# A hand-written issue list carried into the second quarter of an attention + two-layer kernel, with idle transposes ahead of the first work

## The chip, the cores and the metric

One core of a Trainium2 chip runs the kernel. The metric is device time in microseconds (us) of one execution, as the median of three runs; lower is better. The engines are named as in the profile: PE is TensorE's matmul, PEld its weight load, DVE is VectorE, ACT is ScalarE, POOL is GpSimd, SP the engine that issues the DMAs. Each engine executes its own queue in order, and waits on semaphores for the others.

## The reference, cut to what matters

```python
def _attn_ref(x, state):                       # x 4x8x512x64, state 4x8x32x64
    scores = scale * np.matmul(x, state.transpose(0, 1, 3, 2))
    a = softmax(scores)                        # with + 1e-09 in the divisor
    xread = np.matmul(a, state)
    scores2 = scale * np.matmul(state, x.transpose(0, 1, 3, 2))
    a2 = softmax(scores2)
    sread = np.matmul(a2, x)
    return np.concatenate([xread, sread], axis=2)

def _moe_ref(x, w_in, w_out, alpha):           # 2304 tokens, 512 -> 2048 -> 512
    h = x @ w_in
    g = np.maximum(h, 0.0) + alpha * np.minimum(h, 0.0)
    return g @ w_out

def _moe2_ref(x, w_in, w_out):
    h = x @ w_in
    g = np.maximum(h, 0.0) + np.log1p(np.exp(-np.abs(h)))
    return g @ w_out
```

The attention's output, as 2304 rows of 512, goes through the first layer and then the second. The weights arrive as 64-bit floats.

## The kernel before, in words

**Stages.** The 2048 hidden columns of a layer are cut into four quarters of 512 (NQ = 4). A quarter is worked off in blocks: the four batches b = 0 to 3 (512 tokens each, in four column pieces fc of 128 hidden columns) and one block B of 128 rows, the state's rows of all batches. For each piece, `hidden` makes a 128x512 bank of hidden values on PE, `act` applies the layer's function on ACT and DVE and splits the result into a high and a low part (g), and `out_part` multiplies g with the output weights: 12 matmuls of 512 columns, as high x high, low x high and high x low (`mm3`, lines 173 to 175). In the first layer the state is multiplied into the weights first (`sw_products`, line 305), so a hidden bank is 6 matmuls.

**Weights.** 64 weight tiles (`wsrc`: 4 input and 4 output tiles for each quarter and layer) are loaded as 64-bit numbers into staging buffers (`wload`, three buffers and one extra), and turned to 32-bit floats in five operations: a on ACT (two instructions, lines 246 and 247), j, f and v on DVE (lines 251, 257 and 261), g on POOL (line 267). Output tiles are then split into high and low (h on ACT, l on POOL). Tiles 0 to 7 belong to the first quarter, 8 to 15 to the second, 16 to 23 to the third.

**Order.** The attention and the whole first quarter are issued in the order of a list, ORDER, inside `tc.manual_schedule()`. It has 405 steps. A step is a letter with a number; each letter is a small function in `steps()`:

- x, y load the tokens, L loads a weight tile, P loads alpha (all on SP's queue)
- s, S make scores of one or two groups (8 groups of 4 heads), on PE; k copies them (ACT)
- t, m, u, e, z, n, b, c, d turn, reduce, exponentiate, normalise and split the scores for xread; M, E, Z, T, K, R, F, X, W do sread (M and Z on DVE; T, R and X on PE; E, K, F and W on ACT)
- w, p, q multiply the state into input weights (PE) and split the product (ACT, DVE)
- H, A, C, G, D, O, Q are the blocks of the first layer: hidden bank (PE), relu (ACT), prelu (DVE), high part (ACT), low part (DVE), output product (PE), copy of the output (ACT). I, J and H16 are the row block B.

`LOW_POOL` and `SUB_POOL` name the groups whose d and u go to POOL instead of DVE.

All that follows the list, from the second quarter on, is written as loops and ordered by the framework's scheduler, which goes by its own cost model. It may issue an instruction of the loops ahead of steps of the list, on any engine, where it thinks that it is ready sooner. In the loops, `out_part` lags three pieces behind (`LAG`), `wconv` converts one tile ahead where it can, `wprep` (as often as `SPLIT_SECOND` or `SPLIT` name the running piece n) takes a tile over, and `sw_batch` makes the next quarter's products at pieces 10, 13 and 15, and the fourth one at piece 1 of the quarter itself.

PSUM is two pools of four banks: psa (scores, hidden, products) and psb (outputs, and the first two groups' scores).

Of the kernel before, what the change touches and what calls it, by code (L numbers as in the profile page):

```python
# [18 lines left out]
P = 128  # L19
# [26 lines left out]


ORDER = """
x0 P0 L0 L1 x1 x2 L2 L3 s0 a0 k0 j0 a1 t0 M0 f0 E0 m0 s1 T0 k1 j1 e0 v0 K0 f1 L4 g0 z0 v1 a2 n0 t1 L5 g1 Z0
b0 m1 x3 B0 j2 a3 u1 f2 M1 e1 c0 v2 E1 d0 j3 L6 T1 S2 g2 K1 z1 k2 f3 n1 a4 Z1 v3 t2 g3 k3 j4 a5 w00 m2 f4 u2  # L50
w01 b1 p00 j5 p01 H0 v4 f5 L7 g4 e2 x4 q01 c1 H1 A0 d1 v5 h4 C0 a6 l4 w03 z2 G0 j6 A1 n2 D0 p03 C1 g5 O0 f6
G1 a7 D1 v6 h5 b2 g6 H2 t3 c2 j7 l5 h6 m3 H3 A2 f7 l6 C2 u3 O1 G2 v7 A3 e3 D2 g7 C3 z3 G3 O2 h7 D3 n3 d2 l7
M2 x5 y0 L8 b3 E2 w02 q03 c3 O3 p02 d3 Z2 x6 L9 L10 q02 y1 M3 H4 Q3 S4 A4 R0 k4 C4 k5 y2 H5 t4 G4 t5 F0 a8
D4 X0 T2 m5 O4 A5 m4 u5 K2 C5 E3 u4 e5 Z3 e4 j8 H6 G5 z5 W0 a9 R1 D5 n5 R2 z4 A6 O5 F1 b5 n4 F2 C6 c5 j9 G6
b4 X1 D6 X2 c4 H7 W2 d5 d4 W1 f8 T3 A7 H8 M4 K3 C7 E4 O6 v8 G7 Z4 A8 L11 g8 x7 D7 C8 a10 f9 M5 H9 v9 G8 E5
j10 L12 g9 O7 A9 D8 Z5 a11 C9 f10 v10 G9 S6 Q7 j11 L13 g10 y3 y4 D9 H10 f11 v11 k7 O8 k6 g11 t7 a12 t6 m7
a13 m6 O9 u7 A10 u6 e7 C10 e6 z7 G10 H11 z6 n7 D10 R3 n6 A11 b7 T5 y5 F3 L14 T4 C11 c7 X3 b6 O10 K4 d7 W3 M7
c6 j12 K5 d6 M6 G11 E7 D11 R4 E6 f12 H12 Z7 y6 F4 v12 Z6 L15 g12 j13 T6 A12 R5 h12 X4 C12 O11 K6 l12 f13 G12
W4 F5 D12 a14 v13 X5 R6 W5 L16 g13 y7 j14 T7 F6 H13 Q11 f14 v14 H14 L17 g14 A13 K7 C13 X6 O12 A14 G13 C14 W6
D13 G14 D14 R7 H15 F7 h14 l14 X7 A15 w10 h13 C15 W7 O13 l13 G15 p10 D15 q10 I0 J0 H16 A16 C16 G16 D16 w11  # L60
w12 p11 p12 q11 q12
""".split()

BY_PE = (0,)

LOW_POOL = (1, 4, 6, 7)
SUB_POOL = (2, 5)

SPLIT_SECOND = (2, 2, 3, 4, 5, 7, 9, 10, 16)
SPLIT = (1, 2, 4, 5, 7, 9, 10, 16)  # L70

SW_AHEAD = (10, 13, 15)
# [5 lines left out]
def mixer_kernel(  # L78
# [313 lines left out]
    def out_part(m, q, b, fc, g, take=True):  # L392

        gh, gl = g
        if b == B:
            ps = bank(psb)
            for c in range(4):
                f = slice(c * P, (c + 1) * P)
                mm3(ps, gh[:, f], gl[:, f], *weight("o", m, q, c), c == 0, c == 3)
            out_take(m, q, b, 0, ps)  # L400
            return
        if fc == 0:
            for j in range(4):
# [42 lines left out]
    def steps():  # L446
# [228 lines left out]

        @step
        def H(i):
            b, fc = divmod(i, 4)
            if b == 0:
                ps = live["H", i] = bank(psa)  # L680
                for k in range(2):
                    nc.tensor.matmul(
                        ps, sw[0][k][0].f[:, fc * P : (fc + 1) * P], at0_at[k].f, start=k == 0, stop=k == 1
                    )
            elif b < B:
                live["H", i] = hidden(0, 0, b, fc)
# [17 lines left out]

        @step
        def C(i):
            prelu(0, *divmod(i, 4), live["A", i], live["H", i])

        @step
        def G(i):  # L710
# [7 lines left out]

        @step
        def O(i):  # L720
            out_part(0, 0, *divmod(i, 4), live["G", i], take=False)

        @step
        def Q(i):
            for j in range(4):
                out_take(0, 0, i // 4, j, yps[j])

        for x_ in ORDER:
            do[x_[0]](int(x_[1:]))
# [72 lines left out]
```

## Time and profile before

| what | us |
|---|---|
| median of three runs (lowest, highest) | 750.41 (748.25, 751.65) |
| the profiled execution, its own time | 751.67 |
| its span in the trace | 749.9 |
| PE busy in it | 714.9 (95%) |
| DVE, ACT and POOL busy | 448.6, 423.2, 183.9 |

The span runs from the first to the last instruction in the trace. Busy is time in which an engine executes; the granted clock is TensorE's, as a share of 2.4 GHz. A timeline row reads: start, duration, engine, line, operation, what it writes and reads, count, and in square brackets the idle time before it with what ended it.

### The profile page before, as it was taken

To read this page: it belongs to the slowest core of one execution; us is meant where nothing else is said; L and a number is where in the kernel's file an instruction comes from. 1 tells how busy PE (TensorE), PEld (TensorE's weight loads), DVE (VectorE), ACT (ScalarE), POOL (GpSimd) and SP (SyncE) were. 2 spreads that over 40 slices of the span, in tenths; PEclk is the share of its full clock that TensorE was granted. 3 is DMA by queue.
4 is the path that set the end of the run, shared out by engine and by line. 5 is a ranking of instruction groups with operands and counts; after the bars stand their busy time and mean duration, and the time that the engine had idled before them with its cause. 6 is when DMAs were issued, how large, how long until landed. Compare 5 with 4: busy or idle time off the path is not lost.

```text
span 749.9 us, 9339 instructions
## 1 busy us (share of the span) xinstructions
PE 714.9 (95%) x3516; PEld 556.6 (74%) x3516; DVE 448.6 (60%) x697; ACT 423.2 (56%) x765; POOL 183.9 (25%) x150
## 2 busy tenths in 40 slices
PE   3699987699999999999999999999999999999998
PEld 1267764387778777778888888888888888888886
DVE  4989977758668456974596224853267332333433
ACT  4769885735355234754587547864466454544560
POOL 2643433403024002652482004500044000000000
PEclk9799999799999999999999999999999999999999
DMA  7324653304012000320031001310020000001103
GB/s 263 116 81 166 202 171 116 107 2 141 28 49 92 0 1 29 118 79 1 29 112 57 1 0 57 122 48 1 1 59 26 0 1 1 0 1 57 56 15 112
DMA packets 16653, 47.25 MB, mean 63 GB/s; under 512 B 2016, under 2 KB 2016, under 8 KB 16608
## 3 DMA queue, kind: packets, MB, share of 16 engines
q1 hardware_dynamic: 16608, 46.66, 18.9%
q8 instruction: 27, 0.44, 0.2%
q14 instruction: 18, 0.15, 0.1%
HBM read 42.20 MB, written 4.46 MB: 62 GB/s over the span
## 4 chain that ended last, share of the span: by engine, by line
PE 82%; DVE 7%; DMA 4%; ACT 4%; issue 1%; POOL 1%; SPq 0%; ACTq 0%; DVEq 0%
PE pb L174 15%; PE pb L175 15%; PE pb L173 15%; PE pa L173 11%; PE pa L175 11%; PE pa L174 11%; DMA stg<-w1i 2%; DVE top L251 2%; PE pa L341 1%; DVE cnv L261 1%; PE pa L305 1%; ACT exp L246 1%; DMA acc<-xs 1%; ACT top L247 1%; DVE pa L372 1%
## 5 line engine op out<-in xcount | busy, mean ns | idle before, releaser
L386 DVE SCALAR_TENSOR_TENSOR pa<-pa,tmp 128x512 f32<-128x512 f32 x68 | 47.4, 697 | 127.6 <-ACT tmp L385 127.6
L429 DVE TENSOR_TENSOR acc<-pb,acc 128x512 f32<-128x512 f32 x102 | 67.3, 684 | 37.0 <-PE pb L175 37.0
L383 ACT ACTIVATE tmp<-pa 128x512 f32<-128x512 f32 x68 | 40.6, 597 | 85.2 <-PE pa L175 65.7
L267 POOL TENSOR_TENSOR cnv<-top,cnv 128x512 f32<-128x512 bf16 x48 | 59.2, 1233 | 67.8 <-DVE cnv L261 66.4
L251 DVE SCALAR_TENSOR_TENSOR top<-stg,top 128x512 uint16<-128x512 uint16 x63 | 58.1, 922 | 24.8 <-ACT top L247 24.6
L372 DVE SCALAR_TENSOR_TENSOR pa<-tmp,rest,pa 128x512 f32<-128x512 f32 (+1 forms) x80 | 53.4, 669 | 26.5 <-ACT tmp L380 22.9
L246 ACT ACTIVATE exp<-stg 128x512 bf16<-128x512 bf16 x63 | 42.1, 668 | 39.2 <-DMA stg<-w1i 9.7
L380 ACT ACTIVATE tmp<-pa 128x512 f32<-128x512 f32 x51 | 30.0, 595 | 42.2 <-PE pa L175 35.6
L261 DVE SCALAR_TENSOR_TENSOR cnv<-stg,exp 128x512 f32<-128x512 uint32 x48 | 43.8, 913 | 16.3 <-POOL wo5l L182 4.0
L247 ACT ACTIVATE top<-exp,top_bias 128x512 uint16<-128x512 uint16 x64 | 46.0, 719 | 5.0 <-POOL cnv L267 1.5
L385 ACT ACTIVATE tmp<-tmp 128x512 f32<-128x512 f32 x68 | 42.9, 632 | 1.8
L384 ACT ACTIVATE tmp<-tmp 128x512 f32<-128x512 f32 x68 | 43.0, 632 | 1.5
L257 DVE TENSOR_SCALAR exp<-top 128x512 uint16<-128x512 uint16 x64 | 37.4, 584 | 1.1
L179 ACT ACTIVATE g3h<-pa 128x512 fp32r<-128x512 f32 x29 | 17.3, 597 | 20.3 <-DVE pa L372 11.1
L179 ACT ACTIVATE g1h<-pa 128x512 fp32r<-128x512 f32 x29 | 17.3, 597 | 19.6 <-DVE pa L386 11.2
L182 DVE TENSOR_TENSOR g3l<-pa,g3h 128x512 fp32r<-128x512 f32 x29 | 20.0, 689 | 14.0 <-ACT g3h L179 13.7
L179 ACT ACTIVATE g0h<-pa 128x512 fp32r<-128x512 f32 x28 | 16.7, 597 | 20.0 <-DVE pa L386 10.6
L182 DVE TENSOR_TENSOR g2l<-pa,g2h 128x512 fp32r<-128x512 f32 x29 | 19.9, 687 | 12.0 <-ACT g2h L179 12.0
L182 DVE TENSOR_TENSOR g1l<-pa,g1h 128x512 fp32r<-128x512 f32 x29 | 19.9, 688 | 10.2 <-ACT g1h L179 9.8
L179 ACT ACTIVATE g2h<-pa 128x512 fp32r<-128x512 f32 x29 | 17.3, 597 | 13.9 <-DVE pa L386 7.2
L182 DVE TENSOR_TENSOR g0l<-pa,g0h 128x512 fp32r<-128x512 f32 x28 | 19.3, 688 | 9.2 <-ACT g0h L179 8.9
L182 POOL TENSOR_TENSOR wo3l<-cnv,wo3h 128x512 fp32r<-128x512 f32 x4 | 5.2, 1290 | 73.3 <-ACT wo3h L179 73.3
(903 smaller groups left out, 2157.8 us busy)
## 6 DMA issues: line engine op xcount, KB each, us to landing
stg<-w1o SPq DMA_DIRECT2D x16, 511.8 KB, 3.8
stg<-w2i SPq DMA_DIRECT2D x16, 511.8 KB, 3.9
stg<-w2o SPq DMA_DIRECT2D x16, 511.8 KB, 3.3
stg<-w1i SPq DMA_DIRECT2D x15, 511.8 KB, 5.1
acc<-xt SPq DMA_DIRECT2D x16, 256.0 KB, 4.4
out<-acc SPq DMA_DIRECT2D x16, 256.0 KB, 2.0
acc<-xs SPq DMA_DIRECT2D x8, 256.0 KB, 4.6
wo6h<-xs SPq DMA_DIRECT2D x4, 256.0 KB, 5.2
```

Of the source, the lines that this page charges most:

```text
L173: nc.tensor.matmul(ps, lh, rh, start=start, stop=False)
L174: nc.tensor.matmul(ps, lh, rl, start=False, stop=False)
L175: nc.tensor.matmul(ps, ll, rh, start=False, stop=stop)
L179: nc.scalar.activation(h, src, AF.Copy)
L182: eng_l.tensor_tensor(out=l, in0=src, in1=h, op=ALU.subtract)
L246: nc.scalar.activation(e, words(i)[0].bitcast(BF16), AF.Abs)
L247: nc.scalar.activation(t.bitcast(U16), e.bitcast(U16), AF.Relu, bias=top_bias, scale=TOP_SCALE)
L251: nc.vector.scalar_tensor_tensor(out=tu, in0=words(i)[0], scalar=TOP_SIGN, in1=tu, op0=ALU.bitwise_and, op1=ALU.bitwise_or)
L261: nc.vector.scalar_tensor_tensor(out=a, in0=words(i)[1], scalar=REST, in1=parts(i)[1], op0=ALU.mult, op1=ALU.mult)
L267: nc.gpsimd.tensor_tensor(out=a, in0=parts(i)[0], in1=a, op=ALU.add)
L372: nc.vector.scalar_tensor_tensor(out=ps[:, cs], in0=t[:, cs], scalar=a, in1=ps[:, cs], op0=ALU.mult, op1=ALU.add)
L429: nc.vector.tensor_tensor(out=a, in0=ps, in1=a, op=ALU.add)
```

## The change

The list is written anew: 449 steps instead of 405. It goes on past the first quarter's last block to the first batch block of the second quarter: new are H17 to H20 with their A, C, G, D, the outputs O14 to O17, the conversion of tile 15 (a15 to l15), the load L18, and w13, p13, q13 (the second quarter's last product). `BLOCKS` maps a step's number to quarter, block and piece. The loop over the second quarter starts at block 1, piece 4. `SPLIT_SECOND` has eight entries instead of nine, since one tile more is ready.

From the last instruction of the list on each of the five engines, `tc.issue_after` ties what follows: it is issued behind that instruction on that engine. It is an order of issue, not a wait for its end.

A new step N makes a number of 128x128 transposes of the identity into a bank of psb that nobody reads: N12 ahead of s0, N13 ahead of t0, N10 ahead of T0, N4 ahead of s1, N13 ahead of b0, N29 ahead of S2 and N26 ahead of w00, 107 in all. The d of groups 3 and 5 goes to POOL, and the u of group 2 to DVE.

In the diff a part of the old list is left out.

```diff
--- before.py
+++ after.py
@@ -46,27 +46,30 @@
 
 
 ORDER = """
-x0 P0 L0 L1 x1 x2 L2 L3 s0 a0 k0 j0 a1 t0 M0 f0 E0 m0 s1 T0 k1 j1 e0 v0 K0 f1 L4 g0 z0 v1 a2 n0 t1 L5 g1 Z0
-b0 m1 x3 B0 j2 a3 u1 f2 M1 e1 c0 v2 E1 d0 j3 L6 T1 S2 g2 K1 z1 k2 f3 n1 a4 Z1 v3 t2 g3 k3 j4 a5 w00 m2 f4 u2
-w01 b1 p00 j5 p01 H0 v4 f5 L7 g4 e2 x4 q01 c1 H1 A0 d1 v5 h4 C0 a6 l4 w03 z2 G0 j6 A1 n2 D0 p03 C1 g5 O0 f6
...
-W4 F5 D12 a14 v13 X5 R6 W5 L16 g13 y7 j14 T7 F6 H13 Q11 f14 v14 H14 L17 g14 A13 K7 C13 X6 O12 A14 G13 C14 W6
-D13 G14 D14 R7 H15 F7 h14 l14 X7 A15 w10 h13 C15 W7 O13 l13 G15 p10 D15 q10 I0 J0 H16 A16 C16 G16 D16 w11
-w12 p11 p12 q11 q12
+P0 x0 L0 L1 L2 x1 x2 L3 N12 s0 a0 k0 j0 a1 N13 t0 M0 f0 E0 m0 N10 T0 v0 e0 j1 K0 g0 N4 s1 z0 k1 f1 n0 a2 t1
+v1 N13 b0 j2 g1 x3 B0 L4 L5 y0 m1 c0 f2 a3 d0 u1 v2 e1 j3 L6 g2 N29 S2 z1 k2 f3 n1 Z0 k3 v3 a4 b1 g3 t2 c1
+j4 d1 a5 N26 w00 t3 w02 f4 p00 m3 p02 v4 H0 u3 L7 g4 q02 e3 H1 h4 z3 A0 l4 a6 C0 w01 n3 j5 G0 p01 D0 A1 j6
+O0 f5 f6 v5 v6 L8 g5 x4 y1 C1 H2 b3 g6 G1 h5 q01 c3 l5 h6 D1 w03 A2 m2 a7 d3 H3 C2 u2 p03 l6 j7 O1 e2 G2 z2
+a8 D2 n2 A3 f7 O2 b2 v7 c2 C3 g7 d2 R0 G3 q03 x5 h7 x6 L9 y2 F0 l7 X0 D3 H4 W0 M1 M2 E1 H5 j8 A4 E2 Z1 f8 S4
+A5 C4 v8 O3 G4 k4 C5 g8 k5 D4 G5 t5 a9 D5 H6 m5 Q3 t4 u5 H7 j9 m4 e5 O4 A6 f9 z5 A7 v9 n5 u4 T1 g9 C7 e4 T2
+C6 K1 O5 K2 z4 G6 G7 b5 n4 D7 c5 D6 d5 R1 b4 R2 F1 M4 O6 c4 M3 d4 E4 Z2 E3 M5 F2 x7 L10 y3 Z3 y4 E5 Z4 X1 X2
+H8 W1 Z5 W2 T3 A8 O7 K3 C8 G8 D8 a10 H9 Q7 j10 f10 R3 v10 S6 y5 F3 g10 A9 X3 O8 k7 C9 W3 t7 G9 M7 k6 D9 E7
+t6 H10 Z7 m6 H11 m7 A10 M6 T5 C10 A11 O9 E6 u7 C11 K5 e7 Z6 u6 G10 z7 G11 T6 e6 R5 D11 n7 z6 T4 F5 X5 K4 b7
+n6 W5 R4 D10 c7 T7 y6 b6 y7 F4 L11 O10 L12 d7 L13 K7 c6 d6 X4 H12 W4 K6 H13 A12 C12 R6 A13 R7 G12 C13 O11
+a11 D12 a12 j11 f11 G13 v11 H14 F7 D13 L14 g11 F6 Q11 j12 H15 f12 v12 X7 A14 X6 O12 L15 g12 W7 C14 W6 G14
+a14 D14 I0 h12 j14 A15 l12 f14 a13 C15 v14 G15 w11 j13 J0 g14 D15 H16 p11 O13 f13 v13 h14 q11 A16 L16 g13
+L17 C16 l14 h13 O14 a15 l13 G16 j15 w10 D16 f15 O15 v15 p10 L18 g15 q10 H17 Q15 H18 A17 O16 C17 A18 G17 C18
+D17 G18 D18 H19 h15 Q16 l15 H20 A19 C19 O17 A20 G19 C20 D19 G20 D20 w12 w13 p12 p13 q12 q13
 """.split()
 
+BLOCKS = [(0, b, fc) for b in range(B) for fc in range(4)] + [(0, B, 0)] + [(1, 0, fc) for fc in range(4)]
+
 BY_PE = (0,)
 
-LOW_POOL = (1, 4, 6, 7)
-SUB_POOL = (2, 5)
-
-SPLIT_SECOND = (2, 2, 3, 4, 5, 7, 9, 10, 16)
+LOW_POOL = (1, 3, 4, 5, 6, 7)
+SUB_POOL = (0, 5)
+
+SPLIT_SECOND = (5, 6, 7, 8, 9, 10, 11, 16)
 SPLIT = (1, 2, 4, 5, 7, 9, 10, 16)
 
 SW_AHEAD = (10, 13, 15)
@@ -397,8 +400,9 @@
             for c in range(4):
                 f = slice(c * P, (c + 1) * P)
                 mm3(ps, gh[:, f], gl[:, f], *weight("o", m, q, c), c == 0, c == 3)
-            out_take(m, q, b, 0, ps)
-            return
+            if take:
+                out_take(m, q, b, 0, ps)
+            return ps
         if fc == 0:
             for j in range(4):
                 yps[j] = bank(psb)
@@ -463,6 +467,14 @@
 
 
         @step
+        def N(i):
+            if "N" not in live:
+                live["N"] = bank(psb)
+            for _ in range(i):
+                nc.tensor.transpose(live["N"][:, 0:P], ident, ident)
+
+
+        @step
         def L(i):
             assert i == nload[0]
             wload()
@@ -675,15 +687,15 @@
 
         @step
         def H(i):
-            b, fc = divmod(i, 4)
-            if b == 0:
+            q, b, fc = BLOCKS[i]
+            if (q, b) == (0, 0):
                 ps = live["H", i] = bank(psa)
                 for k in range(2):
                     nc.tensor.matmul(
                         ps, sw[0][k][0].f[:, fc * P : (fc + 1) * P], at0_at[k].f, start=k == 0, stop=k == 1
                     )
             elif b < B:
-                live["H", i] = hidden(0, 0, b, fc)
+                live["H", i] = hidden(0, q, b, fc)
             else:
                 live["H", i] = bank(psa)
                 turned(live["H", i], live["J"])
@@ -704,7 +716,7 @@
 
         @step
         def C(i):
-            prelu(0, *divmod(i, 4), live["A", i], live["H", i])
+            prelu(*BLOCKS[i], live["A", i], live["H", i])
 
         @step
         def G(i):
@@ -718,16 +730,19 @@
 
         @step
         def O(i):
-            out_part(0, 0, *divmod(i, 4), live["G", i], take=False)
+            live["O"] = out_part(0, *BLOCKS[i], live["G", i], take=False)
 
         @step
         def Q(i):
+            if i == 4 * B:
+                out_take(0, 0, B, 0, live["O"])
+                return
             for j in range(4):
                 out_take(0, 0, i // 4, j, yps[j])
 
         for x_ in ORDER:
             do[x_[0]](int(x_[1:]))
-        return [(0, 0, *divmod(i, 4), live["G", i]) for i in range(4 * B + 1) if f"O{i}" not in ORDER]
+        return [(0, *x, live["G", i]) for i, x in enumerate(BLOCKS) if f"O{i}" not in ORDER]
 
 
     nc.scalar.preload_act_table_set("natural_log_exp_and_others")
@@ -738,11 +753,15 @@
     with tc.manual_schedule():
         todo = steps()
 
+    last = {x.engine: x for x in nc.cur_bb.bb.instructions}
+    for e in (nc.tensor, nc.vector, nc.scalar, nc.gpsimd, nc.sync):
+        ctx.enter_context(tc.issue_after(last[e.engine]))
+
     gs = []
     for m, q in [(m, q) for m in range(2) for q in range(NQ)][1:]:
         second = (m, q) == (0, 1)
-        blocks = (0, 1, B, 2, 3)
-        n = 0
+        blocks = (1, B, 2, 3) if second else (0, 1, B, 2, 3)
+        n = 4 if second else 0
         for b in blocks:
             for fc in range(4 if b < B else 1):
                 ps = hidden(m, q, b, fc)
@@ -757,7 +776,7 @@
                 if m == 0:
                     if n in SW_AHEAD and q < NQ - 1:
                         sw_batch(q + 1, SW_AHEAD.index(n))
-                    if n == SW_LAST:
+                    if n == SW_LAST and not second:
                         sw_batch(q, B - 1)
                 wprep((SPLIT_SECOND if second else SPLIT).count(n))
                 n += 1
```

## Rows read from the trace of the kernel before

**Rows 1.** Busy by stretch: PE, PEld, DVE, ACT, POOL, granted clock, DMA share, GB/s.

```profile
0.00:40.00 40.00, 22.34 (x113) 8.47 (x114) 28.64 (x54) 25.68 (x45) 17.11 (x21) 0.83 0.52 178
40.00:100.00 60.00, 59.40 (x502) 43.98 (x501) 56.14 (x110) 47.51 (x109) 26.26 (x21) 1.00 0.48 158
100.00:160.00 60.00, 47.12 (x245) 30.99 (x244) 41.61 (x62) 37.71 (x79) 19.90 (x17) 0.86 0.34 106
160.00:260.00 100.00, 100.00 (x474) 76.41 (x473) 69.77 (x112) 47.07 (x81) 21.86 (x17) 1.00 0.18 58
```

**Rows 2.** Timeline of PE: the two longest waits after 100 us.

```profile
132.56 0.80 PE L173 MATMUL pb<-wo0h,g0h 128*128 128x512 f32 x1 [5.77 <-ACT g0h L712]
...
146.82 2.08 PE L173 MATMUL pb<-g1h,wo4h 128*128 128x512 f32 x4 [4.77 <-ACT g1h L179]
```

**Rows 3.** The chain that ended last, in order of time: start, duration, what.

```profile
126.73 4.42 DMA stg<-w1o
...
131.24 0.66 ACT exp L246
131.91 0.61 ACT g0h L712
...
155.58 0.23 PE pa L174
```

**Rows 4.** Timelines of DVE (first row) and ACT, 129 to 147 us.

```profile
129.13 0.69 DVE L261 SCALAR_TENSOR_TENSOR cnv<-stg,exp 128x512 f32<-128x512 uint32 x1
...
140.63 0.68 ACT L246 ACTIVATE exp<-stg 128x512 bf16<-128x512 bf16 x1 [2.76 <-DVE cnv L261]
...
143.34 0.58 ACT L380 ACTIVATE tmp<-pa 128x512 f32<-128x512 f32 x1
...
146.17 0.60 ACT L179 ACTIVATE g1h<-pa 128x512 fp32r<-128x512 f32 x1
```

**Rows 5.** Timeline of PE, first 27 us, and three later rows at full clock.

```profile
4.24 2.60 PE L513 MATMUL pb<-acc,ex0h 64*32 64x512 f32 x8 [4.24 <-DMA acc<-xt]
10.30 1.09 PE L462 MATMUL pb<-ident,ex0l 128*128 128x128 f32 x4 [3.46 <-ACT ex0l L527]
...
13.21 0.66 PE L462 MATMUL pa<-ident,ex0l 128*128 128x128 f32 x4
17.16 1.11 PE L462 MATMUL pb<-ident,acc 128*128 128x128 f32 x4 [3.29 <-POOL acc L568]
22.07 1.12 PE L462 MATMUL pa<-ident,ex1h 128*128 128x128 f32 x4 [3.80 <-ACT ex1h L606]
23.11 1.96 PE L513 MATMUL pa<-acc,ex0h 64*32 64x512 f32 x16
...
26.71 0.63 PE L305 MATMUL pa<-wi1l,ex0h 64*32 64x512 f32 x1
...
55.39 1.09 PE L513 MATMUL pa<-acc,ex0h 64*32 64x512 f32 x16
...
99.35 0.66 PE L462 MATMUL pa<-ident,wi4l 128*128 128x128 f32 x4
99.76 0.48 PE L173 MATMUL pa<-at6h,sw6h 128*128 128x512 f32 x1
```

**Rows 6.** Timeline of DVE from 9 us: its first operation, and M1's maximum.

```profile
9.71 0.69 DVE L251 SCALAR_TENSOR_TENSOR top<-stg,top 128x512 uint16<-128x512 uint16 x1 [8.84 <-ACT top L247]
...
19.50 0.67 DVE L600 TENSOR_REDUCE stn<-ex1h 128x1 f32<-128x512 f32 x1
```

**Rows 7.** The page's groups: count, then busy, mean ns of one, idle before.

```profile
L372 DVE SCALAR_TENSOR_TENSOR pa<-tmp,rest,pa 128x512 f32<-128x512 f32 (+1 forms) x80 | 53.4, 669 | 26.5 <-ACT tmp L380 22.9
L261 DVE SCALAR_TENSOR_TENSOR cnv<-stg,exp 128x512 f32<-128x512 uint32 x48 | 43.8, 913 | 16.3 <-POOL wo5l L182 4.0
L257 DVE TENSOR_SCALAR exp<-top 128x512 uint16<-128x512 uint16 x64 | 37.4, 584 | 1.1
```

**Rows 8.** SP's queue, waits from 60 to 250 us: total, times, longest.

```profile
SPq L483 <- PE pa L630: 7.6, 2, 5.1
```

More of the change, by code (lines that the diff above doesn't have):

```diff
@@ L48 @@
 ORDER = """
-x0 P0 L0 L1 x1 x2 L2 L3 s0 a0 k0 j0 a1 t0 M0 f0 E0 m0 s1 T0 k1 j1 e0 v0 K0 f1 L4 g0 z0 v1 a2 n0 t1 L5 g1 Z0
-b0 m1 x3 B0 j2 a3 u1 f2 M1 e1 c0 v2 E1 d0 j3 L6 T1 S2 g2 K1 z1 k2 f3 n1 a4 Z1 v3 t2 g3 k3 j4 a5 w00 m2 f4 u2
-w01 b1 p00 j5 p01 H0 v4 f5 L7 g4 e2 x4 q01 c1 H1 A0 d1 v5 h4 C0 a6 l4 w03 z2 G0 j6 A1 n2 D0 p03 C1 g5 O0 f6
-G1 a7 D1 v6 h5 b2 g6 H2 t3 c2 j7 l5 h6 m3 H3 A2 f7 l6 C2 u3 O1 G2 v7 A3 e3 D2 g7 C3 z3 G3 O2 h7 D3 n3 d2 l7
-M2 x5 y0 L8 b3 E2 w02 q03 c3 O3 p02 d3 Z2 x6 L9 L10 q02 y1 M3 H4 Q3 S4 A4 R0 k4 C4 k5 y2 H5 t4 G4 t5 F0 a8
@@ L54 @@
[L54 to L58, printed above, removed]
```

## The prediction

> **What bounds the kernel now.** I read the busy table by stretch first, then the timelines where it shows holes, then the chain that ended last. From 160 us on TensorE never stands: it is busy 100.00 of 100 us at granted clock 1.00 [rows 1]. What happens there is fixed by the number of matmuls, which the change leaves alone. From 40 to 100 us, in the middle of the hand-written list, PE is busy 59.40 of 60 us [rows 1]. So time can be won in two places: before 40 us, where PE is busy 22.34 us, and from 100 to 160 us, where it is busy 47.12 of 60 and the granted clock has a mean of 0.86 [rows 1].
>
> In the second place PE's two longest waits make 5.77 + 4.77 = 10.5 of the 12.9 us of idle time [rows 2]. The first ends with g0h, the row block's G16, which is the list's second last step on ACT. The chain shows what G16 stood behind: a weight tile's transfer of 4.42 us, that tile's a step (L246, 131.24), then g0h (131.91) [rows 3]. That tile isn't one of the list's, which ends with tile 14: on DVE the v step at 129.13, into cnv [rows 4], belongs to tile 20 by the order of the tiles, and it too comes ahead of G16. The scheduler had put the loops' conversions among the list's last steps, and in an in-order queue a step that waits for a transfer holds up all behind it. The second wait has the same form: the relu at 143.34 (L380, a line of the loops) stands behind an a step that waited 2.76 us for DVE, and g1h comes at 146.17 [rows 4].
>
> **The change, part by part.**
>
> *Queueing behind the list.* The loops' conversions can no longer stand ahead of H16 to O17's A, C, G, D. What replaces the hole is the list's own order, in which the independent outputs O13 to O16 lie between H16 to H20, so that each g has 2.7 us of matmuls (12 of 0.23 [rows 3]) to hide its chain of A 0.58, C 0.67, G 0.60 and a D that I take to be as long as C, 2.5 us [rows 4, 7]. The stretch in which the old list ran undisturbed shows what such an order gives: 0.6 us idle in 60 [rows 1]. I take the idle time as gone: **12.9 us**. Bounds: 4 us, if only the first hole closes partly, and 12.9.
>
> *The clock.* A mean of 0.86 over 47.12 us of work costs 47.12 x 0.14 = 6.6 us [rows 1]; it fell to its lower level (1.2 GHz) in and behind PE's waits. Without these waits it stays at 2.4 GHz: **6.6 us**; if one wait of some us is left, about half.
>
> *The seam at the list's end.* The last steps on PE are H20, O17, w12, w13. w13 needs two of psa's four banks, which D19 and D20 must free; D20 comes 2.5 us after H20, beside O17's 2.7. Two g chains at once make that nearer 4, and the first hidden bank of the loops must wait for q12. I charge **+2.5 us**; between 0 (the scheduler puts O18 first) and 5 (a whole chain for w13 and one for the bank). Tiles 16 to 18 are loaded by then, and piece 10 of the second quarter, the first that needs tiles 16 to 19, comes six pieces of about 4.1 us (18 matmuls of 0.23) later. The four conversions cost DVE about 2.4 us each (j taken as v, 0.91 each, and f 0.58 [rows 7]) and are hidden by that; if that cover went, they would cost their 10 us. DVE has the room: it is busy 70 of 100 us there [rows 1], and some 12 us of conversions move into it. The tile more in the list, w13, p13, q13 and the fewer `SPLIT_SECOND` entries only move work: nothing.
>
> *The start.* M1 no longer stands ahead of v3 on DVE, which from its first operation at 9.71 to 40 us is busy 28.64 of 30.3 us [rows 1, 6]. M1's maximum is 0.67 [rows 6], with its small second step I say 0.8, and v3, g3 and w00 come that much earlier. S2's 16 records take 1.96 us here and 1.09 at full clock (55.39) [rows 5], T1 moves back behind O4. On the other side alpha's transfer goes ahead of x0, about 0.4 us for s0, and L2 ahead of x1. d3 and d5 leave DVE and u2 comes to it, all about as long as C (0.67 [rows 7]): 0.7 gained. Sum if all goes well: 0.8 + 0.9 + 0.7 - 0.4 = 2.0; I take **1.5**, since a step on DVE is rarely passed on whole.
>
> *The idle transposes.* No row shows a long run of transposes alone. Four took 0.41 us from start to next start at full clock (99.35 to 99.76) and 1.04 at the low one (22.07 to 23.11) [rows 5], so 0.10 or 0.26 each, and the 107 of them 11 or 27 us. The column says 0.83 for the first 40 us, but its first record begins only late: the durations at 10.30 and 22.07 are those of the low clock, and at 13.21 four took 0.66, as at 99.35 [rows 5]. The first 25 fit into waits even when slow: 12 x 0.26 = 3.1 ahead of s0 at 4.24, 13 x 0.26 = 3.4 in the 3.46 ahead of t0 [rows 5]. N29 and N26 decide: 55 transposes lie with S2 between b0 (17.16, some 0.4 us) and the part of w00 that waits longest (26.71, L305 with wi1l) [rows 5], which would come at about 25.9. At 0.10 they take 5.5 and S2 1.1, and fit; at 0.26 they take 14.3 and S2 2.0 in 8.4 us, and w00 and all behind it are 7.9 us late. I take zero, because real work of the list (s1, b0) stands among them, and at 13.21 the clock had risen after little PE work that wasn't transposes; bounds 0 and +7.9.
>
> The Trainium skill speaks against this: TensorE: Matmul & The Clock Gate, Part 4 (PE-mode transpose), says that the full clock doesn't engage for transposes, which do not count as PE being busy in the same way. No run here shows it. By that rule the sum would be 7.9 us higher.
>
> **Sum.** -12.9 - 6.6 + 2.5 - 1.5 = -18.5 us. The profiled execution took 751.67 (span 749.9), so 733.2; it stands 1.26 above the median of the three runs, 750.41, and on that scale the forecast is **732 us**. A check from DVE: it is busy 28.64 + 56.14 + 41.61 = 126 us up to 160 [rows 1]. Less the five conversions of the loops (12 us) that is 114; at the 94% busy share of 40 to 100 us, and from its first operation at 9.71 [rows 6], it needs until 131. The work that follows 156 us in the old trace (155.58 is a hidden bank of the second quarter [rows 3]) could then start 25 us earlier. So DVE leaves room for 18.5, but not for much more.
>
> **The rivals.**
>
> *VectorE becomes the bound.* For: it is busy 94% from 40 to 100 us, and the v step takes 0.69 us at 129.13 but has a mean of 0.91, so something stretches it [rows 1, 4, 7]; two more d steps go to POOL. Against: less is on DVE than before. If its 114 us grow by 10 to 15%, the join comes at 143 to 149 instead of 131, and 7 to 13 us are left: about 740.
>
> *Transposes don't raise the clock*, the case of 7.9 us above: 732 + 7.9 = about 740.
>
> *Slower: late weights in the list's last fifth.* All of L11 to L18 now stand behind y3 to y7 on SP, and y7 waits for R5 to free its buffer. SP has waited for R before, 7.6 us in two waits [rows 8]. a11 stands behind G13; from R5 to H13's end PE has only T4, R4, T7, O10, H12, H13, some 7 us, against a landing of 4.4 [rows 3] behind two more y's. If R5 slips by over 3 us, a11 holds ACT, and the tiles behind it, each loaded into a buffer that an earlier conversion frees, may each hold it again. Five such holds (tiles 11 to 15), each at the price of the one at 132.56, 5.77 [rows 2], are 28.9 us: 732 + 28.9 = 761. With three it is 749. Against: three buffers, so that most landings lie beside other work.
>
> *It does nothing there*: the two holes were latencies of the second quarter's data, and only change their names. 750.
>
> **How the numbers follow.** What a measurement can tell from no change here is about 0.5%, 3.75 us: faster is below 746.7, slower above 754.2. The forecast's case (725 to 737) has 0.52. VectorE as bound, and transposes at low clock, have 0.13 each (737 to 746); both are still faster. With 0.02 for more than 25 us won, faster is 0.80. Doing nothing has 0.07 and the late weights 0.13, of which 0.03 for three holds (749): so the same is 0.10 and slower 0.10. The range 722 to 748 takes in both ends of the unknown costs on the fast side (all bounds good: 750.4 - 12.9 - 6.6 - 2.0 = 729, and DVE's 25 us: 725, less the scatter of 2 to 3 us between runs) and the two middle rivals.
>
> **What would show it.** Right: PE's idle time from 100 to 160 us below 3 us at a clock above 0.95; g0h of the row block no longer behind an L246 that waits for w1o; some PE wait of 1 to 4 us at w13 or the bank behind it; steady work from about 135 us. The start: S2 in about 1.1 us, O0 not later than 35 us. Wrong: a PE wait for ACT or DVE that ends with a late tile 11 to 15; rows of ident transposes at 0.2 us and more between 17 and 30 us with w00 after 30; a DVE without idle time up to the seam while PE waits for prelu or low parts.

## The result and the profile after

| what | before | after |
|---|---|---|
| median of the runs beside each other (lowest, highest), us | 750.37 (748.25, 751.65) | 740.29 (739.10, 740.77) |
| median of a second, longer comparison, us | 750.30 | 740.53 |
| profiled execution, its own time, us | 751.67 | 739.10 |
| its span, us | 749.9 | 737.3 |
| PE busy, us | 714.9 (95%) | 719.7 (98%) |

The ratio is 0.9866, with a 95% interval of 0.9841 to 0.9892, and 0.9871 (0.9851 to 0.9892) in the second comparison: 10 us faster, where 18 had been forecast. The two profiled executions differ by 12.6 us, because the one of before was the slowest of its runs and the one of after the fastest; the sums below are made against the 12.6.

The busy table by stretch of the changed kernel, to be held against [rows 1] (columns: the stretch; its length; PE, PEld, DVE, ACT and POOL busy with their counts; the granted clock; the share of the DMA engines; GB/s):

```profile
0.00:40.00 40.00, 34.19 (x223) 21.35 (x223) 29.68 (x53) 23.98 (x41) 18.08 (x20) 1.00 0.56 186
40.00:100.00 60.00, 55.70 (x458) 40.91 (x458) 48.17 (x99) 44.22 (x107) 22.44 (x19) 1.00 0.37 122
100.00:160.00 60.00, 58.77 (x351) 42.30 (x349) 44.85 (x72) 41.52 (x81) 17.51 (x14) 1.00 0.31 102
160.00:200.00 40.00, 37.81 (x195) 27.25 (x194) 38.42 (x61) 25.02 (x44) 16.64 (x13) 1.00 0.40 131
```

The hole from 100 to 160 us is closed: PE is busy 58.77 of 60 us instead of 47.12, at a clock of 1.00 instead of 0.86. But two stretches that were full have opened. From 40 to 100 us PE stands 4.30 us instead of 0.60, and from 160 to 200 us 2.19 instead of 0. Further on nothing differs: in the last 540 us of the two profiles PE is busy 536.1 and 535.9 us.

PE's timeline has the waits themselves (columns as in the rows of before):

```profile
50.72 0.33 PE L658 MATMUL pa<-ident,acc 128*128 128x128 f32 x1 [0.79 <-ACT acc L654]
69.55 0.50 PE L177 MATMUL pb<-g2l,wo2h 128*128 128x512 f32 x1 [1.09 <-DVE g2l L729]
81.89 0.33 PE L658 MATMUL pa<-ident,wo5h 128*128 128x128 f32 x1 [0.84 <-ACT wo5h L654]
116.19 0.63 PE L466 MATMUL pa<-ident,tmp 128*128 128x128 f32 x4 [0.78 <-ACT sw2h L679]
128.84 0.39 PE L176 MATMUL pb<-wo0h,g0h 128*128 128x512 f32 x1
134.28 0.39 PE L176 MATMUL pb<-g1h,wo4h 128*128 128x512 f32 x1
137.09 0.61 PE L308 MATMUL pa<-wi2h,ex0h 64*32 64x512 f32 x1
172.67 0.62 PE L308 MATMUL pa<-wi1h,ex0h 64*32 64x512 f32 x2 [1.31 <-DVE g2l L185]
191.05 0.50 PE L176 MATMUL pa<-at6h,sw6h 128*128 128x512 f32 x1 [0.88 <-DVE g1l L185]
```

The rows at 128.84 and 134.28 are those that waited 5.77 and 4.77 us [rows 2]; neither waits now. The one at 137.09 is the list's end, w12 and w13: no wait there either. In place of two long waits stand many short ones, none over 1.6 us: for a softmax step on ACT (X0 and X3, at 50.72 and 81.89), for a low part on DVE (69.55, 172.67, 191.05), or for a split on ACT (116.19).

ACT's timeline shows what the tie did:

```profile
135.96 0.60 ACT L724 ACTIVATE g0h<-pa 128x512 fp32r<-128x512 f32 x1 [0.33 <-DVE pa L375]
140.19 1.25 ACT L249 ACTIVATE exp<-stg 128x512 bf16<-128x512 bf16 x2
143.83 0.60 ACT L383 ACTIVATE tmp<-pa 128x512 f32<-128x512 f32 x1 [1.17 <-PE pa L178]
148.69 0.67 ACT L249 ACTIVATE exp<-stg 128x512 bf16<-128x512 bf16 x1 [0.93 <-DMA stg<-w1i]
```

G20 (135.96) is the list's last g. The loops' first conversion on ACT comes behind it at 140.19, and the transfer that a conversion waits for (148.69) now holds up no step of the list, as it did at 131.24 and 131.91 [rows 3].

The transfer was not the only hold in the kernel before. DVE's timeline there shows that the row block's last prelu (L372) stood behind a conversion too, a j step of 1.61 us:

```profile
129.99 1.61 DVE L251 SCALAR_TENSOR_TENSOR top<-stg,top 128x512 uint16<-128x512 uint16 x1
131.53 0.34 DVE L372 SCALAR_TENSOR_TENSOR pa<-tmp,rest,pa 128x128 f32<-128x128 f32 x1
```

This prelu ended at 131.87, so g0h, which needs it, could have come only 0.04 us earlier than 131.91 without the transfer. The loops' conversions filled both queues, ACT's and DVE's.

### The profile page after: what moved, and what is told of

Same layout as the page of the kernel before. It is cut to its first block, busy times and chain, and to the rows that moved or that the text cites. A ratio compares the mean times of both kernels' runs of the same rounds, so it can differ in the third digit from the quotient of the medians.

```text
span 737.3 us, 9532 instructions
## 1 busy us (share of the span) xinstructions
PE 719.7 (98%) x3623; PEld 565.3 (77%) x3623; DVE 447.6 (61%) x696; ACT 423.4 (57%) x765; POOL 187.1 (25%) x151
## 4 chain that ended last, share of the span: by engine, by line
PE 79%; DVE 11%; DMA 4%; ACT 3%; issue 2%; POOL 1%; SPq 0%; DVEq 0%; ACTq 0%
PE pb L176 14%; PE pb L177 14%; PE pb L178 14%; PE pa L176 11%; PE pa L178 11%; PE pa L177 11%; DMA stg<-w1i 3%; DVE top L254 2%; PE pa L344 1%; PE pa L308 1%; DVE pa L375 1%; DVE exp L260 1%; DVE cnv L264 1%; ACT exp L249 1%; ACT top L250 1%
## 5 line engine op out<-in xcount | busy, mean ns | idle before, releaser
L386 ACT ACTIVATE tmp<-pa 128x512 f32<-128x512 f32 x68 | 40.7, 598 | 85.2 <-PE pa L178 65.7
L270 POOL TENSOR_TENSOR cnv<-top,cnv 128x512 f32<-128x512 bf16 x48 | 60.7, 1266 | 61.3 <-DVE cnv L264 61.3
L249 ACT ACTIVATE exp<-stg 128x512 bf16<-128x512 bf16 x63 | 41.9, 668 | 38.5 <-DMA stg<-w1i 11.5
L383 ACT ACTIVATE tmp<-pa 128x512 f32<-128x512 f32 x47 | 27.5, 594 | 30.5 <-PE pa L178 23.9
L182 ACT ACTIVATE g1h<-pa 128x512 fp32r<-128x512 f32 x28 | 16.7, 595 | 19.3 <-DVE pa L389 11.2
L185 DVE TENSOR_TENSOR g3l<-pa,g3h 128x512 fp32r<-128x512 f32 x28 | 19.3, 688 | 12.1 <-ACT g3h L182 11.9
L182 ACT ACTIVATE g2h<-pa 128x512 fp32r<-128x512 f32 x28 | 16.7, 596 | 11.8 <-DVE pa L389 7.2
```

The source lines that it names most:

```text
L182: nc.scalar.activation(h, src, AF.Copy)
L185: eng_l.tensor_tensor(out=l, in0=src, in1=h, op=ALU.subtract)
L249: nc.scalar.activation(e, words(i)[0].bitcast(BF16), AF.Abs)
L270: nc.gpsimd.tensor_tensor(out=a, in0=parts(i)[0], in1=a, op=ALU.add)
```

## The experiments

In the edits and diffs below, `...` marks what is left out. For each profiled execution the span splits into parts that sum to it: the first 40 us, and PE's idle and busy time behind them. The first 40 us hold the idle transposes and the low clock of the start, so "idle" and "busy" count from 40 us on; a fall of the clock lies in "busy".

| run | span | PE idle behind 40 us | PE busy behind 40 us | ratio to before (95%) |
|---|---|---|---|---|
| before | 749.9 | 17.3 | 692.5 | |
| after | 737.3 | 11.8 | 685.5 | 0.9866 (0.9841 to 0.9892) |
| after2 | 738.7 | 12.4 | 686.4 | 0.9871 (0.9851 to 0.9892) |
| no_n | 741.5 | 13.8 | 687.7 | 0.9870 (0.9837 to 0.9903) |
| no_n2 | 737.8 | 11.2 | 686.7 | 0.9880 (0.9862 to 0.9899) |
| loose | 743.7 | 13.2 | 690.5 | 0.9929 (0.9904 to 0.9955) |
| old_tied | 742.4 | 11.7 | 690.7 | 0.9886 (0.9854 to 0.9918) |
| old_fill | 741.7 | 13.6 | 688.2 | 0.9925 (0.9889 to 0.9960) |
| pace | 739.1 | 12.1 | 687.0 | 0.9882 (0.9864 to 0.9900) |
| early | 738.2 | 11.6 | 686.7 | 0.9856 (0.9834 to 0.9878) |
| pace_tied | 738.4 | 11.3 | 687.1 | 0.9863 (0.9835 to 0.9891) |
| tuned | 739.9 | 13.0 | 686.9 | 0.9870 (0.9839 to 0.9901) |
| both | 741.6 | 13.5 | 688.1 | 0.9882 (0.9854 to 0.9909) |

About 3.7 us of each idle figure lie behind 700 us, in all kernels alike. The run n_long, a single execution, stands below. Profiles of one kernel differ by up to 3.7 us (no_n and no_n2), so ratios decide and the columns say where.

### The change taken apart

**no_n**: the changed kernel without its idle transposes.

```diff
-... L3 N12 s0 a0 k0 j0 a1 N13 t0 M0 f0 E0 m0 N10 T0 ...
+... L3 s0 a0 k0 j0 a1 t0 M0 f0 E0 m0 T0 ...
```

> The changed kernel without its 107 idle transposes. Theory 1 (the transposes hold TensorE's clock up): the granted clock falls to 0.50 somewhere between 10 and 40 us again, S2 takes 1.9 us instead of 1.3, and the time is 2 to 4 us above the changed kernel's 740.3, so 742 to 744. Rival (the start is set by VectorE and the transfers, a faster TensorE only waits longer): within 1 us of 740.3, whatever the clock does.

Measured: 741.47 us, ratio 0.9870, the same as with them, although the granted clock did fall (0.87 in the first 40 us). The run is repeated beside the changed kernel below.

**loose**: the changed kernel without the tie, so that the scheduler may put the loops' work among the list's steps.

```diff
-    last = {x.engine: x for x in nc.cur_bb.bb.instructions}
-    for e in (nc.tensor, nc.vector, nc.scalar, nc.gpsimd, nc.sync):
-        ctx.enter_context(tc.issue_after(last[e.engine]))
```

> The changed kernel without the ties that queue the loops behind the list. Theory 1 (the loops' conversions ahead of the list's last steps made the holes of the kernel before): TensorE waits of several us for ScalarE come back between 105 and 150 us, time 746 to 752. Rival (the longer list is enough, since the row block now has 20 us of other list work behind it): 740 to 742, no wait over 2 us there.

Measured: 746.41 us, ratio 0.9929: about half of the gain is gone. Its table by stretch, around the list's end:

```profile
100.00:160.00 60.00, 56.49 (x330) 37.87 (x328) 48.53 (x75) 45.40 (x90) 26.45 (x20) 1.00 0.42 142
160.00:200.00 40.00, 38.45 (x180) 27.71 (x181) 32.63 (x53) 18.79 (x32) 7.58 (x6) 1.00 0.25 79
```

POOL is busy 26.45 us there instead of 17.51: conversions are back among the list's steps. PE stands 3.51 us in these 60 instead of 1.23. The 5 us holes of before do not return, so theory 1 had the time right and not the waits. That the new list has more independent work between its blocks may be why; no run shows it.

The larger part of the loss is busy time: over the whole span PE is busy 723.6 us, against 719.7 in the changed kernel. The scheduler put the loops' outputs into the middle of w12 and w13 on PE as well. In the changed kernel eight of their 64x32 matmuls start within 0.04 us of each other (from 137.09 on) and take 0.61 us each, side by side. In loose two of them go ahead alone, and an output of the loops comes behind them:

```profile
140.63 1.04 PE L308 MATMUL pa<-wi2h,ex0h 64*32 64x512 f32 x2
141.60 0.73 PE L176 MATMUL pb<-g2h,wo5h 128*128 128x512 f32 x2
```

At 145.33 the same happens once more. From 110 to 205 us the 112 matmuls of L308 keep PE busy for 10.73 us, where they do so for 8.43 in the changed kernel: 2.3 of the 4 us. Some 1.5 us more come from a fall of the clock between 35 and 40 us, which runs with the tie show too (last section), so that isn't an effect of the tie.

**old_tied**: the kernel before, with the tie alone.

```diff
         todo = steps()
 
+    last = {x.engine: x for x in nc.cur_bb.bb.instructions}
+    for e in (nc.tensor, nc.vector, nc.scalar, nc.gpsimd, nc.sync):
+        ctx.enter_context(tc.issue_after(last[e.engine]))
```

> The kernel before with the ties alone: old list, loops queued behind it. Theory 1 (queueing is most of the gain): the 5.8 us wait for the row block's g goes, and the time falls by 5 to 9 us, to 741 to 745. Rival (the old list ends too early: its last g chains have nothing beside them, and the conversions of tiles 15 on, now all behind it, come late for the second quarter): one or two waits of 3 us and more at the seam, time 748 to 755.

Measured: 743.00 us beside 751.60, ratio 0.9886. Its PE timeline at the places of [rows 2] and behind:

```profile
121.92 0.61 PE L305 MATMUL pa<-wi3h,ex0h 64*32 64x512 f32 x1 [1.77 <-DVE g0l L717]
133.95 0.50 PE L173 MATMUL pb<-wo0h,g0h 128*128 128x512 f32 x1
136.82 0.39 PE L173 MATMUL pb<-g1h,wo4h 128*128 128x512 f32 x1
177.67 0.71 PE L305 MATMUL pa<-wi1h,ex0h 64*32 64x512 f32 x2 [2.81 <-DVE g1l L182]
```

Both holes are gone with three lines of the change, and the idle time behind 40 us (11.7) is already that of the whole change (11.8). The row block's four prelus, which take from 128.41 to 131.87 between conversions in the kernel before, here run in one piece of 1.53 us from 118.98 on. The tie is the part that works on the holes. The clock still falls a few times in this kernel (0.97 from 40 to 160 us, 0.96 from 160 to 200, some 5 us of work), which is why its busy time (690.7) stays some 5 us above that of after.

**old_fill**: the kernel before, with idle transposes at the same places (N12 ahead of s0, N13 ahead of t0, N24 ahead of b0, N29 ahead of T1) and no tie.

```diff
-x0 P0 L0 L1 x1 x2 L2 L3 s0 a0 k0 j0 a1 t0 M0 ...
+x0 P0 L0 L1 x1 x2 L2 L3 N12 s0 a0 k0 j0 a1 N13 t0 M0 ...
```

> The kernel before with idle transposes ahead of s0 (12), t0 (13), b0 (24) and T1 (29), nothing else changed. Theory 1: the clock stays at 1.00 through the first 40 us, and S2 and the slow matmuls of O0 give back 2 to 3 us: 747 to 748.5. Rival (VectorE and transfers set the start): 749.5 to 751.

Measured: 743.94 us, below both expectations, ratio 0.9925 with a wide interval (0.9889 to 0.9960).

```profile
129.64 0.79 PE L173 MATMUL pb<-wo0h,g0h 128*128 128x512 f32 x1 [5.80 <-ACT g0h L720]
141.10 1.19 PE L173 MATMUL pb<-g1h,wo4h 128*128 128x512 f32 x4 [1.28 <-ACT g1h L179]
```

The first hole stays as it was, 5.80 us, and comes 2.9 us earlier. Here no transfer stands right ahead of g0h; it waits for the last prelu, which stands behind a j step of 1.61 us on DVE (127.08):

```profile
128.61 0.34 DVE L372 SCALAR_TENSOR_TENSOR pa<-tmp,rest,pa 128x128 f32<-128x128 f32 x1
128.99 0.60 ACT L720 ACTIVATE g0h<-pa 128x512 fp32r<-128x512 f32 x1 [1.11 <-DVE pa L372]
```

The second hole shrank from 4.77 to 1.28 us. The steps of the list are the same, but the order of the loops' work isn't: on ACT the relu (L380) comes here right behind the a step (137.71, 138.29), while in the kernel before four steps stood between the two (140.63, 143.34). So the transposes in the list changed the order that the scheduler gave to the loops, and the run doesn't show what the transposes alone are worth.

By the medians, the new list with its transposes (loose) gives 5.2 us, the tie 8.6 and old_fill 7.7 (5.6 by its ratio), against 10 for the whole change: they remove the same time, and do not add up.

### The transposes, and the pieces behind the list

**after2** is the changed kernel once more.

> The changed kernel once more, as the reference for the three beside it on the same chip: 1.1 to 1.6% below the kernel before.

**no_n2** is no_n once more.

> The changed kernel without the idle transposes once more, beside the changed kernel. Theory 1 (they are worth what the clock gives in the first 40 us): 2.5 to 4.5 us above the changed kernel in the same call, as TensorE's first output product of the second quarter (g1 with wo4) came 4.3 us later in the first profile. Rival: within 1 us.

Measured: 740.53 and 741.54 us; the intervals of the ratios, 0.9871 and 0.9880, overlap almost wholly. By the two pairs of medians the 107 transposes are worth 1.0 and 1.2 us in the new list, which the scatter doesn't tell from nothing. They do raise the clock. In no_n2 PE's rows at the start are those of the low clock:

```profile
11.20 1.09 PE L466 MATMUL pb<-ident,ex0l 128*128 128x128 f32 x4 [3.46 <-ACT ex0l L539]
17.56 1.11 PE L466 MATMUL pb<-ident,acc 128*128 128x128 f32 x4 [1.39 <-POOL acc L580]
30.95 1.52 PE L694 MATMUL pa<-wo4h,sw0h 128*128 128x512 f32 x2
```

and in the changed kernel they are not:

```profile
1.36 2.82 PE L474 MATMUL pb<-ident 128*128 128x128 f32 x12 [1.36 <-POOL ident masks.py:199]
7.46 3.04 PE L474 MATMUL pb<-ident 128*128 128x128 f32 x13
16.89 0.66 PE L466 MATMUL pb<-ident,acc 128*128 128x128 f32 x4 [0.65 <-POOL acc L580]
17.38 3.33 PE L474 MATMUL pb<-ident 128*128 128x128 f32 x29
20.64 1.34 PE L525 MATMUL pa<-acc,ex0h 64*32 64x512 f32 x16
21.91 3.06 PE L474 MATMUL pb<-ident 128*128 128x128 f32 x26
28.43 1.13 PE L694 MATMUL pa<-wo4h,sw0h 128*128 128x512 f32 x2
```

The first 25 transposes take 0.23 us each, the last 55 some 0.12 (3.33 / 29). H0 starts at 28.43 instead of 30.95. DVE (third of the busy times) has no time left in the changed kernel from 20 to 60 us:

```profile
20.00:40.00 20.00, 17.25 (x121) 8.73 (x119) 19.83 (x35) 13.54 (x25) 12.04 (x10) 1.00 0.44 149
40.00:60.00 20.00, 19.14 (x128) 12.63 (x128) 19.76 (x35) 15.29 (x33) 9.87 (x9) 1.00 0.48 169
```

It is busy 39.6 of 40 us, and 38.9 without the transposes. How much of PE's gain lasts differs between the profiles. With transposes (after, after2) H0 comes at 28.43 and 29.12, and O17 at 134.28 and 135.82; without (no_n2, no_n) H0 comes at 30.95 and 31.54, and O17 at 134.92 and 138.62. That PE waits for DVE for what it wins at the start is likely, but not shown.

**pace**: the second quarter's conversions spread wider, and none taken ahead.

```diff
-SPLIT_SECOND = (5, 6, 7, 8, 9, 10, 11, 16)
+SPLIT_SECOND = (4, 5, 6, 8, 10, 12, 14, 16)
...
-                wconv()
+                if not second:
+                    wconv()
```

> The changed kernel with the loops' conversions spread over the second quarter: no conversion ahead of time, tiles 16 to 23 at pieces 4, 5, 6, 8, 10, 12, 14, 16. Theory 2 (behind the list VectorE is the bound, since eight conversions crowd it between 142 and 190 us): TensorE's waits of 1.3 and 0.9 us at 172 and 190 us go, VectorE's busy share from 160 to 200 us falls from 96% to below 88%, time 1.5 to 4 us below the changed kernel. Rival (the order of the quarter is what it is, and conversions made later are then late for the third quarter): no gain, or waits for a weight tile from 190 us on, 0 to 5 us above.

Measured: 741.13 us, ratio 0.9882 (0.9864 to 0.9900). The run tells nothing of its question: the scheduler gave every engine the same order as in the changed kernel. Where a call stands in the loops does not set where its instructions are issued.

**early**: tiles 16 and 17 are converted inside the list, in DVE's idle time ahead of its end, and leave the second quarter.

```diff
-... p10 L18 g15 q10 H17 Q15 H18 ...
+... p10 L18 g15 q10 a16 j16 H17 Q15 f16 v16 L19 g16 H18 ...
...
-SPLIT_SECOND = (5, 6, 7, 8, 9, 10, 11, 16)
+SPLIT_SECOND = (7, 8, 9, 10, 11, 16)
```

> The changed kernel with the conversions of tiles 16 and 17 put into the list, where VectorE stands from 125 to 139 us, and L19 and L20 behind them. Theory 2: as with the spread conversions, 1.5 to 3 us below the changed kernel, and VectorE's idle time from 120 to 140 us falls from 9.5 to about 6 us. Rival (an a step ahead of the last relus holds ScalarE up, as in the kernel before): a new TensorE wait of 1 us or more between 125 and 140 us, no gain.

Measured: 739.99 us, ratio 0.9856. DVE's idle time from 120 to 140 us fell from 9.5 to 5.7 us, and no new PE wait came there. PE's idle time from 160 to 200 us fell from 2.17 to 1.35, and DVE's busy time there from 38.40 to 36.32 of 40 us. The median is 0.5 us below that of after2 beside it, and the intervals overlap almost wholly: a gain isn't shown.

### Closing the waits one by one

**n_long** asks for the price of the transposes themselves, in a single execution.

```diff
-j4 d1 a5 N26 w00 t3 ...
+j4 d1 a5 N130 w00 t3 ...
```

> The changed kernel with 130 instead of 26 idle transposes ahead of w00, so that TensorE does nothing but these for some 15 us. Theory 1 (transposes hold the clock as other work does): the granted clock stays at 1.00 right through, the 130 take 0.117 us each, 15 us, and the time grows by 10 to 12 us, to about 751. Rival (they do not count as activity): the clock falls to 0.50 within the run of transposes, most of them take about 0.23 us, 25 us and more in all, time above 757.

Measured: 750.19 us. The PE timeline:

```profile
22.57 14.41 PE L474 MATMUL pb<-ident 128*128 128x128 f32 x130
36.92 0.61 PE L308 MATMUL pa<-wi0h,ex0h 64*32 64x512 f32 x1
38.80 1.12 PE L694 MATMUL pa<-wo4h,sw0h 128*128 128x512 f32 x2
```

130 transposes took 14.41 us, 0.111 each, to the last at the full clock, and the work behind them ran at it at once. The span is 9.7 us above that of after2, H0 is 9.7 us later (38.80 against 29.12), and 104 more transposes are 11.5 us: they lie on the path as soon as they are longer than the wait that they fill. The Trainium skill, in TensorE: Matmul & The Clock Gate, Part 4 (PE-mode transpose), says that the full clock doesn't engage for transposes, since they do not count as PE being busy in the same way. This trace disagrees: at the price of the low clock, 0.23, the 130 would have taken 30 us. That section of the Trainium skill speaks of TensorE's transpose mode and gives its figures for bf16. These transposes are of fp32, and the profile doesn't show whether that mode is on.

**pace_tied** does what pace meant to: in the second quarter each piece's conversions are tied on DVE and ACT behind that piece's own steps.

```diff
-                wprep((SPLIT_SECOND if second else SPLIT).count(n))
+                with ExitStack() as behind:
+                    if second:
+                        last = {x.engine: x for x in nc.cur_bb.bb.instructions}
+                        for e in (nc.vector, nc.scalar):
+                            behind.enter_context(tc.issue_after(last[e.engine]))
+                    wprep((SPLIT_SECOND if second else SPLIT).count(n))
```

> The changed kernel with the loops' conversions really spread: in the second quarter each tile (pieces 4, 5, 6, 8, 10, 12, 14, 16) is queued on VectorE and ScalarE behind that piece's own steps. The run called pace left the engines' orders as they were, but for names, and told nothing. Theory 2 (behind the list VectorE is crowded by conversions made ahead of time): TensorE's idle time from 160 to 200 us falls from 2.2 us to below 0.8, VectorE's busy time there from 38.5 to below 35 of 40 us, and the time is 1 to 3 us below the changed kernel's 0.987 of the kernel before: 0.983 to 0.986. Rival (the waits move on to the third quarter, for which the tiles then come late): TensorE idle from 200 to 280 us, ratio 0.987 or more.

Measured: 741.42 us, ratio 0.9863. Its table by stretch:

```profile
160.00:200.00 40.00, 40.00 (x206) 29.35 (x205) 27.57 (x46) 20.64 (x36) 9.24 (x8) 1.00 0.20 66
200.00:260.00 60.00, 59.16 (x272) 44.68 (x271) 55.12 (x86) 35.15 (x61) 24.34 (x18) 1.00 0.32 106
```

The 2.2 us of idle time from 160 to 200 us are gone, with DVE at 27.57 of 40 us; 0.84 us came back behind 200 us, where the conversions now crowd DVE (55.12 of 60). The whole idle time behind 40 us is 11.3 us against 11.8 in after and 12.4 in after2. Such a gain, 1 us, is below what the runs can tell, and the median shows none.

**tuned** moves three steps of the list for which PE waited in its middle (D6 ahead of D7, X0 behind H4, X3 behind C9) and puts N12 ahead of O0.

```diff
-C6 K1 O5 K2 z4 G6 G7 b5 n4 D7 c5 D6 d5 ...
+C6 K1 O5 K2 z4 G6 D6 G7 b5 n4 D7 c5 d5 ...
```

> The changed kernel with four places of the list mended: D6 ahead of b5 and D7, X0 behind H4, X3 behind O8, and 12 idle transposes ahead of O0. Theory 3 (the middle of the new list loses some 4 us because single small steps stand too early on TensorE, not because VectorE has too much work): the waits of 0.8 us at X0, 1.1 at O6 and 0.8 at X3 go, TensorE's idle time from 40 to 100 us falls from 4.3 to below 2.5 us, time 1.5 to 3 us below the changed kernel: ratio 0.983 to 0.985. Rival (VectorE sets the pace from 20 to 60 us and what is saved at one wait is waited for at the next): idle time as before within 1 us, ratio 0.986 to 0.988.

Measured: 741.65 us, ratio 0.9870. TensorE's idle time from 40 to 100 us rose from 4.30 to 6.17 us, against both expectations. The waits moved instead of going:

```profile
51.40 0.47 PE L176 MATMUL pa<-at2h,sw2h 128*128 128x512 f32 x1 [1.11 <-DVE sw6l L685]
73.41 0.33 PE L658 MATMUL pa<-ident,acc 128*128 128x128 f32 x1 [1.54 <-ACT acc L654]
94.45 0.66 PE L466 MATMUL pa<-ident,wi5l 128*128 128x128 f32 x4 [2.25 <-DVE g3l L729]
```

The waits of 0.79, 1.09 and 0.84 us of the changed kernel are gone. But the one at 73.41 has 1.54 us where it had 0.37, the one at 94.45 has 2.25 where it had 0.43, and the clock fell once just behind it (0.89 from 90 to 105 us).

**both** puts tuned and pace_tied together.

> The mended list and the spread conversions together. If theories 2 and 3 hold, their gains add: 3 to 5 us below the changed kernel, ratio 0.980 to 0.983. If only one holds, 0.983 to 0.986.

Measured: 742.63 us, ratio 0.9882 (0.9854 to 0.9909). From 160 to 200 us PE is busy 40.00 of 40, as in pace_tied; from 40 to 100 us it stands 7.23 us, more than in tuned (6.17), and the total (13.5) is above that of after. The gains don't add. No version clearly beats the changed kernel.

## Why the prediction was right, and where it was not

The measured time, 740.3, lies in the range and on the right side; the forecast's case (725 to 737) did not come true, and it is the width of the range (722 to 748) that covers the 8 us between forecast and measurement. Its terms, against the profiled pair:

**Queueing behind the list, -12.9, and the seam, +2.5: together -10.4, measured -5.5** (17.3 to 11.8 in the table of splits). The mechanism was right: both holes went, in old_tied by the tie alone, and no g of the list stands behind a conversion that waits for a transfer. One reading under it was too narrow. The prediction put the first hole down to the transfer ahead of the a step at 131.24; DVE's queue alone would have held g0h until 131.87, and in old_fill the hole is as long without a transfer right ahead of g0h. Conversions stood in the queues of both engines.

The size was off. From 100 to 160 us 11.65 of the 12.9 us came, and the seam cost nothing instead of 2.5. But 3.7 us were given back from 40 to 100 us and 2.2 from 160 to 200. The step that failed is the sentence "The stretch in which the old list ran undisturbed shows what such an order gives: 0.6 us idle in 60", and with it "I take the idle time as gone". The new list was made anew from end to end, so that stretch was no longer the old one, and PE waits there for single steps of 0.4 to 1.1 us. A full DVE alone doesn't explain them: 3.45 of the 4.30 us lie from 60 to 100 us, where DVE (third of the busy times) is busy for less time than before. Before (first row) and after:

```profile
60.00:100.00 40.00, 39.55 (x370) 30.79 (x369) 38.59 (x78) 34.67 (x85) 18.35 (x15) 1.00 0.50 165
60.00:100.00 40.00, 36.55 (x331) 28.28 (x331) 28.41 (x65) 28.92 (x75) 12.57 (x11) 1.00 0.31 99
```

Behind the list lay a second omission. I had the old loops' conversions only removed from 100 to 160 us, and called four conversions behind the seam hidden. But the loops convert ahead where they can: the conversions of fifteen tiles (16 to 30, not the eight that the expectation of pace counts) start between 140 and 190 us, DVE is busy 38.42 of 40 us from 160 to 200, and PE waits for low parts. In pace_tied DVE is busy 27.57 us there, and the waits are gone.

**The clock, -6.6, and the start, -1.5: together -8.1, measured -7.0** (692.5 to 685.5 busy; to 686.4, -6.1, in after2). The clock was priced rightly: taken in steps of 2 us, the low clock costs the kernel before 6.4 us of PE's work from 40 to 210 us, and the changed kernel nothing there. So the start brought 0.6 us at most. H0 comes 1.1 us earlier (28.43 instead of 29.56), O0 only 0.5 (34.73 instead of 35.26), and in after2 it comes at 35.41, later than before.

That leaves 5.5 + 7.0 = 12.5 of the 12.6 us; the rest is rounding. Of the forecast's 18.5 us 5.9 are missing, 4.9 of them idle time.

**The idle transposes, 0: right in the sum.** They ran at 0.12 us where 55 of them decide, S2 took 1.34 us against the 1.1 that I had, and nothing was late. (The 107 at 0.26 each would have made 28 us, not 27; no term uses it.) But the sum holds without them too (no_n, no_n2), so they were not the condition for the clock behind the list: without them it is 1.00 there as well.

**The rivals.** *VectorE becomes the bound* gave 740 for the time, but not by its mechanism: the list was done at 139 us, not at 143 to 149, and DVE's busy time from 40 to 160 us fell from 97.8 to 93.0. That its price is the measured time is chance; what of it held is the full DVE from 160 to 200 us. *Transposes don't raise the clock* is refuted by n_long. *Late weights in the list's last fifth* did not happen: no PE wait from 117 us to the list's end. *It does nothing there* is refuted by the two rows without a wait.

**What would show it.** PE's idle time from 100 to 160 us is 1.23 us (forecast: below 3) at a clock of 1.00; O0 comes at 34.73 (forecast: not later than 35), but at 35.41 in after2. A wait of 1 to 4 us at w13 was named as a sign of being right, and is missing. PE works without a wait from 117 to 171 us, where steady work had been expected from about 135, and then waits twice more.

**What stays open.** Pace_tied and early each lowered the idle time behind the list, and no median followed beyond scatter. Whether some 4 us of idle time in the list's middle could be had by another order isn't known: the one try (tuned) moved it. What the new list is worth beyond the tie isn't shown either: old_tied (0.9854 to 0.9918) and the whole change (0.9841 to 0.9892) overlap.

## What to carry to other kernels

Where a hand-written order is followed by work that a scheduler places, tie the two at the seam first, on every engine: on the old list three lines gave 8.6 us where the whole rewrite gave 10. Without the tie, an edit of the list can also change the order of what follows it, as in old_fill, and then the run prices both. Do not count a hole as won in full: when a list is made anew, its undisturbed stretches are new too, and here 0.6 us of idle time in 60 became 4.3. Parts that remove the same idle time do not add up, so price each of them alone and all together.

## What had not been expected of the hardware

A run of nothing but fp32 transposes of 128x128 keeps the granted clock at its upper level (2.4 GHz): 130 in 14.41 us, 0.111 each, against 0.23 in the first 25 of the changed kernel.

The clock column can read 1.00 where the clock is low, ahead of its first record. In no_n2 the first 40 us have this row:

```profile
0.00:40.00 40.00, 25.35 (x113) 8.25 (x114) 27.85 (x51) 22.80 (x38) 17.30 (x19) 1.00 0.53 179
```

while four transposes at 17.56 us took 1.11 us, the duration of the low clock, and 0.66 in the changed kernel. The durations are the safer reading.

The clock fell once between about 36 and 40 us in the profiles of loose, pace and early (0.66 from 35 to 40 us in loose and pace, 0.68 in early), and not in those of after, after2 and pace_tied, although all have the same wait of about 1.6 us ahead of O0; by an estimate from these figures (4.38 us of work at 0.66 in loose) this costs some 1.5 us, and it is part of the scatter. With N12 ahead of O0 (tuned) it stayed at 1.00 there and fell at 95 us instead, behind the longer wait.
